# An attention and two expert-layer kernel: gates applied where results are added up, tokens stationary in the down product, sums of h left in PSUM, products of one visit interleaved

## The chip, the cores and the metric

The kernel runs on one core of a Trainium2 chip. The metric is the device time of one execution in microseconds (us); several runs were made and their median is given. A profile of one further execution gives a span, from the first to the last instruction. Engines are named as in the profile: PE is the matrix engine (its weight loads are PEld), DVE the vector engine, ACT the scalar engine, POOL the GpSimd engine, SP the engine that issues the DMAs.

## The reference

Random-feature attention, then eight dense experts gated by a Sinkhorn matrix P, then one wide layer with a swish-like activation. All is float32; 2304 tokens, width 512.

```python
x = attention(q, k, v, omega)                 # (2304, 512)
P = exp(x @ w_gate - max); 8 rounds of row and column normalization
out = 0
for e in range(8):                            # w1[e]: 512 x 1024, w2[e]: 1024 x 512
    h = np.maximum(x @ w1[e], 0.0)
    out += P[:, e:e+1] * (h @ w2[e])
h = out @ w_in                                # 512 x 2048
g = h * (1 / (1 + np.exp(-1.702 * h)))
return g @ w_out                              # 2048 x 512
```

## The kernel before

**Stages.** First attention is computed, with the products of expert 0 (done in the plain way) mixed in. Then come 54 visits. A visit takes one pair of 256-column chunks of an expert's hidden width (c is 0 or 1) and one block j of 768 tokens: 7 experts x 2 pairs x 3 blocks make 42 visits of the first layer (l = 0), and 4 pairs x 3 blocks make 12 of the second (l = 1). Every float32 operand is split in a high and a low part, so each product is three matmuls (high x high, high x low, low x high).

**Inside a visit.** Both products, up (x times w1 gives h) and down (h times w2), are done by a scheme of the Strassen-Winograd kind: 7 block products in place of 8, with sums of blocks made before and after. Q = 384 is half a block of tokens, FC = 256 a chunk. The up part (`up_fast`) makes 7 products per chunk, each 6 matmuls over 384 columns into a PSUM bank, `prod` (L1132). First products are copied by ACT to an SBUF buffer (`ring`, L1142), later ones are added to that buffer by DVE (L1147), the gate and the ReLU are applied (`gate`, L1159, times a row of gates broadcast in `gb`), and sums of the four results are made buffer by buffer (`mix`, L636 by way of `tt`). `operand` splits each of seven h operands: ACT casts the high part (L1179), DVE or POOL subtracts it for the low part (L636). The down part is `down_t` in layer 0 (L1245: w2 is stationary, h moves, 384 columns; DVE adds to `acc` in L1255) and `down_n` in layer 1 (L1269: h is stationary, w2 moves, 256 columns; L1288, or ACT's copy L1284 for the first visit of a block). In layer 1 `gate` is a sigmoid on ACT (L1168) and a product (L1174 or L636).

**The side work.** x operands come by DMA from DRAM (`load_x`, `xo`), weights come raw, are summed and split by ACT and POOL (`load_w1`, `load_w2`, `split`). w_in and w_out arrive as float64; `double_piece` turns 64 pieces of 256 columns into float32 by six DVE instructions (L1069 to L1085) and one addition, spread over the first layer. Between the layers `y_operands` makes the seven x operands of the second layer out of `acc`.

**The order.** All of this after the attention is recorded as operations with keys that they read and write. A planner (`Plan`) simulates the engines with a cost for each operation and emits every engine's instructions in the order of its simulation. Its main PE operations stay in the order in which they were recorded; for operations marked VP it also decides whether DVE or POOL does them. On the chip each engine then runs its list strictly in order and waits at semaphores. In before the visits are recorded one after the other: chunk 0 up, chunk 1 up, down.

Of the kernel before, what the change touches and what calls it, by code (L numbers as in the profile page):

```python
# [10 lines left out]
F32 = mybir.dt.float32  # L11
# [13 lines left out]
class Plan:  # L25
# [7 lines left out]
    LAT = 0.13  # L33
    BELOW = 5.0
# [58 lines left out]
    def run(self):  # L93
# [12 lines left out]
        while done < len(self.ops):  # L106
# [8 lines left out]
            for e in ("X", "PE", "DVE", "POOL", "ACT", "SP"):  # L115
# [57 lines left out]
def tile_performer_sinkhorn_moe(  # L173
# [25 lines left out]
    P = 128  # L199
# [399 lines left out]
    scr_g = dram.tile([NTILE * E, P], F32, name="scr_g")  # L599
# [11 lines left out]

    def rec(eng, dur, fn, r=(), w=(), **kw):
# [3 lines left out]
        else:  # L616
            plan.add(eng, dur, fn, r, w, **kw)
# [4 lines left out]
    def dve_us(n):  # L622
        return 0.12 + 0.00136 * n

    def ps_us(n):
        return 0.17 + 0.00103 * n
# [22 lines left out]
    acc_t = [t.rearrange("p (k n) -> p k n", n=SUP) for t in ACC]  # L649
    acc_n = [t.rearrange("p (t d) -> p t d", d=DM) for t in ACC]  # L650

    def acc_q(j, d, th):
        return acc_t[j][:, d, th * Q : (th + 1) * Q]

    def acc_keys(j):
        return [("acc", j, d, th) for d in range(NK) for th in range(2)]
# [74 lines left out]
    def e0_visit(c, j, halves, begins, ends, nxt, after, first):  # L731
# [32 lines left out]
        for th in halves:  # L764
            fs = range(NF) if th == 0 else range(NF - 1, -1, -1)
            for d in range(NK):
                o, key = free_bank(py_banks, "py")
                for m, f in enumerate(fs):

                    def fn(e, o=o, d=d, f=f, m=m, i=hs[th, f]):  # L770
                        e0_mm(o(), [w[:, f, d * P : (d + 1) * P] for w in EW], EH[i], 6, 3 * m, e)
# [3 lines left out]
                        "PE", 3 * MM, fn,  # L775
                        [("ew", f, 0), ("ew", f, 1), ("eh", i, 0), ("eh", i, 1)], [key], main=True,
                    )
                    if m:
                        a, k = acc_q(j, d, th), ("acc", j, d, th)
                        if first:  # L780
                            rec("ACT", act_us(Q), lambda e, a=a, o=o: nc.scalar.copy(a, o()), [key], [k])
                        else:
                            rec(
                                "DVE", ps_us(Q),
                                lambda e, a=a, o=o: e.tensor_tensor(out=a, in0=o(), in1=a, op=ALU.add),
                                [key, k], [k],
                            )
                        if d:
# [6 lines left out]
                    yield 3 * MM  # L795
# [26 lines left out]
    def sinkhorn():  # L822
# [643 lines left out]
```

## Time and profile before

| | |
|---|---|
| time, median of 3 runs | 2373.74 us (2370.9 to 2382.63) |
| time of the profiled execution | 2373.05 us |
| its span | 2371.3 us |
| busy PE / DVE / ACT / POOL | 89% / 83% / 39% / 65% of the span |
| mean granted PE clock | 0.965 |
| DMA | 440.76 MB, mean 186 GB/s |

The difference between time and span is what lies around the program. Busy shares are averages over stages of different kind. Matmuls are pipelined and overlap in the profile, so a busy PE isn't a PE at its peak; what a matmul takes in a dense run is read from how many start in a stretch.

### The profile page before, as it was taken

How to read it: one execution, taken by the hardware profiler on the slowest of the kernel's cores; microseconds unless marked ns; L12 is line 12 of the kernel's file. 1: busy time of each engine (PE TensorE's matmuls, PEld its weight loads, DVE VectorE, ACT ScalarE, POOL GpSimd, SP SyncE). 2: the span in 40 equal slices, each digit the busy share in tenths (PEclk: the TensorE clock that was granted, in tenths of full speed). 3: DMA queues.
4: the chain of work that ended last, by engine and by line, in shares of the span. 5: the costliest groups of instructions: out<-in, count | busy, mean ns of one | idle time of the engine just before them, and what ended most of it. 6: DMA issues, size and time to landing. Idle time of an engine off the chain costs nothing. (4 is left out here: it accounts for less than half of the span.)

```text
span 2371.3 us, 35013 instructions
## 1 busy us (share of the span) xinstructions
PE 2102.4 (89%) x12248; PEld 2005.1 (85%) x12248; DVE 1979.5 (83%) x3132; ACT 929.3 (39%) x2026; POOL 1538.9 (65%) x1341
## 2 busy tenths in 40 slices
PE   8999997788888888889888889888899877899988
PEld 8999987787878888788888888788888877888988
DVE  7666579989998998989898998988987988687777
ACT  6655533232333342333333243333333355535433
POOL 3212036767776776768776676857687877678776
PEclk9999998899999999999999999999999989999999
DMA  7333168464654654665555555645664678345444
GB/s 153 92 79 90 45 237 228 172 219 149 231 194 170 234 201 165 228 191 189 222 201 179 222 198 178 232 182 183 222 198 162 242 260 278 126 190 211 166 170 147
DMA packets 259919, 440.76 MB, mean 186 GB/s; under 512 B 74512, under 2 KB 199072, under 8 KB 259744
## 3 DMA queue, kind: packets, MB, share of 16 engines
q1 hardware_dynamic: 259744, 438.53, 54.0%
q8 instruction: 97, 1.59, 0.3%
q14 instruction: 78, 0.64, 0.1%
HBM read 392.25 MB, written 46.21 MB: 185 GB/s over the span
## 5 line engine op out<-in xcount | busy, mean ns | idle before, releaser
L1132 PE MATMUL bank<-xo,w 128*128 128x384 f32 x4536 | 846.8, 342 | 123.7 <-DVE ring L1147 68.9
L1132 PEld LDWEIGHTS bank<-xo,w 128*128 128x128 f32 x4536 | 796.0, 191 | 163.0 <-DVE ring L1147 88.7
L1245 PE MATMUL bank<-h,w 128*128 128x384 f32 x3528 | 675.5, 347 | 82.4 <-DVE h L636 38.5
L636 POOL TENSOR_TENSOR h<-ring,h 128x384 fp32r<-128x384 f32 x471 | 561.5, 1205 | 271.5 <-ACT h L1179 198.6
L1245 PEld LDWEIGHTS bank<-h,w 128*128 128x128 f32 x3528 | 635.0, 195 | 118.5 <-DVE h L636 51.9
L1179 ACT CAST h<-ring 128x384 fp32r<-128x384 f32 x756 | 378.9, 513 | 541.3 <-DVE ring L636 248.7
L636 POOL TENSOR_TENSOR w<-raw,w 128x512 fp32r<-128x512 f32 (+1 forms) x216 | 349.6, 1632 | 60.2 <-ACT w L1048 60.1
L1142 ACT COPY ring<-bank 128x384 f32<-128x384 f32 x324 | 154.5, 478 | 555.8 <-PE bank L1132 546.7
L1255 DVE TENSOR_TENSOR acc<-bank,acc 128x384 f32<-128x384 f32 x588 | 301.9, 548 | 51.6 <-PE bank L1245 50.2
L636 DVE TENSOR_TENSOR h<-ring,h 128x384 fp32r<-128x384 f32 x285 | 293.9, 1044 | 7.2 <-ACT h L1179 5.4
L636 DVE TENSOR_TENSOR ring<-ring,ring 128x384 f32<-128x384 f32 (+1 forms) x285 | 292.2, 1029 | 2.0 <-POOL ring L636 0.2
L1147 DVE TENSOR_TENSOR ring<-bank,ring 128x384 f32<-128x384 f32 x324 | 177.7, 550 | 123.1 <-PE bank L1132 117.6
L636 POOL TENSOR_TENSOR ring<-ring,ring 128x384 f32<-128x384 f32 (+1 forms) x171 | 208.8, 1224 | 50.8 <-DVE ring L1159 26.3
L1159 DVE SCALAR_TENSOR_TENSOR ring<-ring,gb 128x384 f32<-128x384 f32 x252 | 232.3, 924 | 10.8 <-DMA gb<-scr_g 8.4
L1269 PE MATMUL bank<-w,h 128*128 128x256 f32 x1512 | 203.8, 297 | 32.5 <-DVE h L636 18.5
L1269 PEld LDWEIGHTS bank<-w,h 128*128 128x128 f32 x1512 | 198.1, 204 | 38.2 <-DVE h L636 20.5
L636 POOL TENSOR_TENSOR raw<-raw 128x256 f32<-128x256 f32 x262 | 217.2, 844 | 16.1 <-DMA raw<-in_moe_w_dram 12.5
L696 POOL TENSOR_TENSOR egl<-raw,egh 128x512 fp32r<-128x512 f32 x32 | 41.1, 1303 | 204.2 <-ACT egh L693 194.4
L1048 ACT CAST w<-raw 128x768 fp32r<-128x768 f32 (+1 forms) x216 | 148.2, 691 | 62.3 <-PE bank L1132 28.6
L1288 DVE TENSOR_TENSOR acc<-bank,acc 128x256 f32<-128x256 f32 x216 | 77.9, 414 | 31.3 <-PE bank L1269 24.3
L387 ACT ACTIVATE feat<-pj,nb 128x128 f32<-128x128 f32 x272 | 73.9, 386 | 66.8 <-DVE nb L383 66.6
L636 POOL TENSOR_TENSOR ring<-ring,gb 128x384 f32<-128x384 f32 x35 | 37.5, 1077 | 71.2 <-ACT gb L1168 71.2
(245 smaller groups left out, 2232.1 us busy)
## 6 DMA issues: line engine op xcount, KB each, us to landing
xo<-sx SPq DMA_DIRECT2D x378, 768.0 KB, 7.5
raw<-in_moe_w_dram SPq DMA_DIRECT2D x288, 128.0 KB, 2.4
sx<-ring SPq DMA_DIRECT2D x48, 192.0 KB, 3.4
gb<-scr_g SPq DMA_DIRECT2D x24, 384.0 KB, 8.0
raw<-in_moe_w_dram SPq DMA_DIRECT2D x16, 512.0 KB, 3.4
f64r<-in_moe_w_in_dram SPq DMA_DIRECT2D x32, 256.0 KB, 3.9
f64r<-in_moe_w_out_dram SPq DMA_DIRECT2D x32, 256.0 KB, 2.9
sx<-acc SPq DMA_DIRECT2D x42, 192.0 KB, 4.4
```

The source lines that it names most:

```text
L387: nc.scalar.activation(f[:, h, :], pvs[h // 4][:, h % 4, :], AF.Exp, bias=nb[:, h : h + 1])
L636: lambda e: e.tensor_tensor(out=out(), in0=a(), in1=b(), op=op),
L1048: lambda e, a=a, b=b: nc.scalar.copy(T[w, c, 0][:, a:b], r[:, a:b]), raws, [(w, c, g, 0)],
L1132: nc.tensor.matmul(o(b), T["w1", c, a][:, slot, kk], T["xo"][x][:, y, kk], start=start and kk == 0 and n == 0, stop=kk == 1 and n == 2, sk ...
L1142: rec("ACT", act_us(Q), lambda e: nc.scalar.copy(RT(i), o(b)), [("b", b)], [("ring", i)])
L1147: lambda e: e.tensor_tensor(out=RT(i), in0=o(b), in1=RT(i), op=ALU.add),
L1159: lambda e: e.scalar_tensor_tensor(out=RT(i), in0=src(), scalar=0.0, in1=g(), op0=ALU.max, op1=ALU.mult),
L1179: rec("ACT", act_us(Q), lambda e: nc.scalar.copy(T["h", c, a, 0], RT(i)), [("ring", i)], [("h", c, a, 0)])
L1245: nc.tensor.matmul(bank[i][:, :Q], T["w2", c, x][:, slot, d * P : (d + 1) * P], T["h", c, a, y], start=start and c == 0 and m == 0, stop=c ...
L1255: lambda e, q=q, i=i: e.tensor_tensor(out=q, in0=bank[i][:, :Q], in1=q, op=ALU.add),
L1269: nc.tensor.matmul(bank[i][:, u], T["h", c, a, x][:, t * P : (t + 1) * P], T["w2", c, y][:, slot], start=start and t % 2 == 0 and c == 0 a ...
L1288: lambda e, q=q, i=i, u=u: e.tensor_tensor(out=q, in0=bank[i][:, u], in1=q, op=ALU.add),
```

## The change

- **Gates** are no longer multiplied into h. In layer 0 ReLU is all that h gets; the gate of a token multiplies the result when it is added to `acc` (one DVE instruction with the gate as a per-partition factor). `gb`, its DMAs (`load_gates`, 24 of 384 KB) and the broadcast are gone. Expert 0's gate is applied by ACT.
- **Down product**: tokens are stationary in both layers, `acc` holds tokens by rows throughout. The old `down_t` goes; 126 matmuls of 256 columns stand in place of its 84 of 384. Expert 0's down product is turned as well (512 columns). `y_operands` therefore transposes `acc` on PE first, and is cut in three units per block.
- **Sums of h stay in PSUM**: ACT copies the first product to the next bank (PSUM to PSUM) and matmuls accumulate on it; DVE adds bank and ring into a bank; the casts and the low parts read the bank; three of the sums read a bank and one ring. One sum per chunk stays ring by ring.
- **First down product**: ACT copies its three results to the banks where the second one accumulates, and DVE adds only the accumulated sums.
- **Woven order**: `up_fast` and `down` are generators; the two chunks' products alternate, the first down turn comes before the last up product, and the last down turn of a visit comes after the first up product of the next.
- **float64 pieces**: 32 of 512 columns in place of 64 of 256, the final addition always on POOL.
- **The planner's costs** change (DVE instructions on SBUF dearer, hand-over time 0.17).

```diff
-    LAT = 0.13
-    BELOW = 5.0
+    LAT = 0.17
+    BELOW = 2.5
...
     def dve_us(n):
-        return 0.12 + 0.00136 * n
+        return 0.17 + 0.0022 * n
...
     def gate_rows(j):
-        for d in range(NK):
-            a = acc_t[j][:, d, :]
...
+        for t in range(ST):
+            a, g = acc_n[j][:, t], pg[:, ST * j + t, 0:1]
+            rec(
+                "ACT", act_us(DM), lambda e, a=a, g=g: nc.scalar.activation(a, a, AF.Copy, scale=g),
...
+    def y_operands(j, u, b0):
+        plan.haste = plan.clock + (2.0, 3.0, 3.0)[u], (0.14, 0.14, 0.2)[u]
+        for b, t in ((b0, u), (b0 + 1, u + 3)):
+            def fn(e, b=b, t=t):
+                for kk in range(NK):
+                    nc.tensor.transpose(
+                        bank[b][:, kk * P : (kk + 1) * P], acc_n[j][:, t, kk * P : (kk + 1) * P], ident
+                    )
...
     def up_fast(l, p, j, c):
-        le, ri, pc = ((0, 1, 2), (3, 4, 2))[c]
-        m1, u2, m5, r21, s1, s2 = range(6 * c, 6 * c + 6)
+        le, ri, pc, q = ((0, 1, 2, 7), (3, 4, 2, 7))[c]
+        r11, u2, r22, n3, s1, s2 = range(6 * c, 6 * c + 6)
...
         prod(le, 0, 0, True)
-        copy(m1, le)
-        prod(pc, 2, 3, True)
-        add(m1, pc)
-        gate(m1, 0)
-        operand(A11, m1)
-        prod(le, 3, 2, False)
-        copy(u2, le)
+        act(lambda: o(pc), lambda: o(le), [("b", le)], [("b", pc)])
+        yield
         prod(ri, 1, 1, True)
-        copy(m5, ri)
+        act(lambda: RT(r22), lambda: o(ri), [("b", ri)], [("ring", r22)])
+        for slot in (3, 2) if c == 0 else (2, 3):
+            if slot == 3:
+                prod(le, 3, 2, False)
+                act(lambda: RT(u2), lambda: o(le), [("b", le)], [("ring", u2)])
+                continue
+            prod(pc, 2, 3, False)
+            if l:
+                swish(pc)
+            operand(A11, bank_of(pc), True, r11)
+        yield
         prod(le, 5, 4, False)
-        add(m5, le)
-        gate(m5, 1)
+        dve(bank_of(q), bank_of(le), ring_of(r22), ALU.add)
+        if l:
+            swish(q)
+        operand(A22, bank_of(q), True, r22)
+        tt(lambda: RT(s2), lambda: RT(r22), lambda: RT(r11), ALU.subtract, Q, [("ring", r22), ("ring", r11)], [("ring", s2)])
         prod(ri, 4, 5, False)
-        add(u2, ri)
-        gate(u2, 0)
-        operand(A12, u2)
+        dve(bank_of(ri), bank_of(ri), ring_of(u2), ALU.add)
+        if l:
+            swish(ri)
+        operand(A12, bank_of(ri), True)
+        yield
         prod(le, 6, 6, False)
-        gate(r21, 1, le)
-        mix(s1, r21, m5, ALU.add)
-        mix(r21, r21, m1, ALU.subtract)
-        mix(s2, r21, m5, ALU.add)
+        if l:
+            swish(le)
+        mixed(s2, le, s2, ALU.add)
+        mixed(s1, le, r22, ALU.add)
+        mixed(n3, le, r11, ALU.subtract)
...
-        mix(u2, u2, s2, ALU.subtract)
-        operand(S4, u2)
-        operand(A22, m5)
+        mixed(u2, ri, s2, ALU.subtract)
+        operand(S4, ring_of(u2))
...
+    PLACES = {
+        "C": ((5, 0), (5, 1), (6, 0)),
+        "D": ((0, 0), (2, 0), (1, 0)),
+        "E": ((7, 0), (7, 1), (6, 1)),
+    }
...
+                if n == 0:
+                    d = PLACES["D"][t][0]
+                    rec(
+                        "ACT", act_us(FC),
+                        lambda e, i=i, d=d, u=u: nc.scalar.copy(bank[d][:, 0:FC], bank[i][:, u]),
+                        [("b", i, half)], [("b", d)],
+                    )
+                    continue
...
+                    g = pg[:, ST * j + m, e : e + 1]
+                    rec(
+                        "DVE", ps_us(FC),
+                        lambda e, q=q, i=i, u=u, g=g: e.scalar_tensor_tensor(
+                            out=q, in0=bank[i][:, u], scalar=g, in1=q, op0=ALU.mult, op1=ALU.add
+                        ),
...
     def all_visits():
+                ups = [up_fast(l, p, j, c) for c in range(2)]
                 load_x(l, j)
+                next(ups[0])
+                for _ in last or ():
+                    pass
...
+                next(ups[0])
+                next(ups[1])
+                next(ups[0])
+                next(ups[1])
+                for _ in ups[0]:
+                    pass
...
+                next(ups[1])
+                last = down(l, e, j, l and p == 0, l and not more)
+                next(last)
+                for _ in ups[1]:
+                    pass
...
+                for _ in range(len(TURNS[l]) - 2):
+                    next(last)
```

What the planner makes of it in a middle visit of layer 0. DVE in before, from the sum of one product to the sums of h (names: `bank` PSUM, `ring` SBUF, `gb` gates, `h031` the low part of operand 3 of chunk 0, `f64r` and `f64w` the float64 work):

```order
L1147 TENSOR_TENSOR ring6_3911<-bank2_3889,ring6_3911 128x384 [waits PE_49,Activation_49]
L636 TENSOR_TENSOR h031_4789<-ring4_3909,h030_4788 128x384 [waits Activation_49]
L1159 SCALAR_TENSOR_TENSOR ring6_3911<-ring6_3911,gb_4500 128x384 [waits DVE_49]
L1069 TENSOR_SCALAR f64w_4502<-f64r_4501 128x256 [waits DMAHW1_49]
L1073 SCALAR_TENSOR_TENSOR f64w_4502<-f64r_4501,f64w_4502 128x256 [waits DVE_49]
L1147 TENSOR_TENSOR ring8_3913<-bank3_3890,ring8_3913 128x384 [waits PE_49,Activation_49]
L1076 TENSOR_SCALAR f64w_4502<-f64r_4501 128x256 [waits DMAHW2_49]
L1159 SCALAR_TENSOR_TENSOR ring8_3913<-ring8_3913,gb_4500 128x384 [waits DVE_49]
L1147 TENSOR_TENSOR ring7_3912<-bank4_3891,ring7_3912 128x384 [waits PE_49]
L1159 SCALAR_TENSOR_TENSOR ring9_3914<-bank3_3890,gb_4500 128x384 [waits PE_49]
L1159 SCALAR_TENSOR_TENSOR ring7_3912<-ring7_3912,gb_4500 128x384 [waits DVE_49]
L636 TENSOR_TENSOR ring10_3915<-ring9_3914,ring8_3913 128x384 [waits DVE_49]
```

DVE in the change at the same place (L1173 adds bank and ring into a bank, L1211 makes a low part out of a bank, L1184 a sum out of a bank and a ring, `stage` is the float64 work, now 512 wide):

```order
L1173 TENSOR_TENSOR bank7_3773<-bank0_3766,ring2_3786 128x384 [waits DVE_49,PE_49]
L1082 TENSOR_SCALAR stage_4180<-stage_4180 128x512 [waits DMAHW0_49,Pool_49]
L1211 SCALAR_TENSOR_TENSOR h061_4560<-bank7_3773,h060_4559 128x384 [waits Activation_49]
L1173 TENSOR_TENSOR bank1_3767<-bank1_3767,ring1_3785 128x384 [waits PE_49]
L1086 SCALAR_TENSOR_TENSOR stage_4180<-stage_4180 128x512 [waits DVE_49]
L1211 SCALAR_TENSOR_TENSOR h101_4564<-bank2_3768,h100_4563 128x384 [waits Activation_49]
L1211 SCALAR_TENSOR_TENSOR h011_4550<-bank1_3767,h010_4549 128x384
L1184 SCALAR_TENSOR_TENSOR ring4_3788<-bank0_3766,ring2_3786 128x384 [waits PE_49]
L1184 SCALAR_TENSOR_TENSOR ring5_3789<-bank0_3766,ring5_3789 128x384 [waits Pool_49]
L1184 SCALAR_TENSOR_TENSOR ring3_3787<-bank0_3766,ring0_3784 128x384
L1173 TENSOR_TENSOR bank7_3773<-bank3_3769,ring8_3792 128x384 [waits DVE_49,PE_49]
```

Nearly every row of DVE now has one operand in PSUM, and the gate's rows are gone.

PE in before, from the last product of a visit (`xo6`) to the first down product, which follows at once:

```order
L1132 MATMUL bank3_3890<-xo6_3904,w111_4499 128x384
L1132 MATMUL bank3_3890<-xo6_3904,w110_4498 128x384
L1245 MATMUL bank5_3892<-h000_4782,w200_4780 128x384
L1245 MATMUL bank5_3892<-h001_4783,w200_4780 128x384 [waits Pool_49]
L1245 MATMUL bank5_3892<-h000_4782,w201_4781 128x384
L1245 MATMUL bank6_3893<-h000_4782,w200_4780 128x384
L1245 MATMUL bank6_3893<-h001_4783,w200_4780 128x384
L1245 MATMUL bank6_3893<-h000_4782,w201_4781 128x384
L1245 MATMUL bank7_3894<-h030_4788,w200_4780 128x384
```

PE in the change, from the end of the first down turn (chunk 0, `h001`) over the last up product to the second down turn (chunk 1, `h100`):

```order
L1294 MATMUL bank6_3772<-w200_4545,h001_4548 128x256
L1152 MATMUL bank3_3769<-xo6_3783,w110_4178 128x384 [waits DVE_49]
L1152 MATMUL bank3_3769<-xo6_3783,w111_4179 128x384
L1152 MATMUL bank3_3769<-xo6_3783,w110_4178 128x384 x2
L1152 MATMUL bank3_3769<-xo6_3783,w111_4179 128x384
L1152 MATMUL bank3_3769<-xo6_3783,w110_4178 128x384
L1294 MATMUL bank5_3771<-w210_4561,h100_4563 128x256
L1294 MATMUL bank5_3771<-w211_4562,h100_4563 128x256
L1294 MATMUL bank5_3771<-w210_4561,h101_4564 128x256
```

The first down turn has moved ahead of the last up product.

PE in the change two turns later, where the third tile of turn `h03` goes into the second half of bank 6, whose first half ACT copies away:

```order
L1294 MATMUL bank7_3773<-w200_4545,h030_4553 128x256
L1294 MATMUL bank7_3773<-w201_4546,h030_4553 128x256
L1294 MATMUL bank7_3773<-w200_4545,h031_4554 128x256
L1294 MATMUL bank6_3772<-w200_4545,h030_4553 128x256 [waits Activation_49]
L1294 MATMUL bank6_3772<-w201_4546,h030_4553 128x256
L1294 MATMUL bank6_3772<-w200_4545,h031_4554 128x256
L1294 MATMUL bank0_3766<-w200_4545,h010_4549 128x256
```

The two halves of bank 6 belong to different sums, and yet the later one waits for the reader of the earlier.

## Rows read from the trace of the kernel before

**Rows 1.** Windows: the four stretches of visits; busy us, clock, DMA share, GB/s.

```profile
core 0: us, PE busy (x) PEld busy (x) DVE busy (x) ACT busy (x) POOL busy (x), PEclk, DMA share, GB/s
420.00:545.50 125.50, 101.10 (x501) 94.52 (x500) 111.84 (x154) 36.75 (x73) 87.12 (x70) 0.90 0.53 187
545.50:1938.00 1392.50, 1223.82 (x6558) 1159.17 (x6557) 1256.94 (x1895) 478.93 (x963) 1006.37 (x869) 0.97 0.57 201
1938.00:2098.60 160.60, 132.58 (x841) 126.63 (x841) 117.34 (x163) 81.47 (x182) 118.36 (x101) 0.93 0.61 218
2098.60:2366.80 268.20, 250.74 (x1682) 246.54 (x1680) 202.86 (x341) 118.90 (x248) 197.12 (x169) 0.96 0.46 172
```

**Rows 2.** Source line L1132: min/median/max ns, first and last start; idle until (us, times).

```profile
L1132 PE MATMUL bank<-xo,w x4536: 331/334/689, 420.0 to 2350.1; 128*128 128x384 f32 x198
...
  DMA xo<-sx: 1.7, 2
```

**Rows 3.** Timeline of three visits: start us, us, engine, line, names, count.

```profile
1014.35 12.71 PE L1132 MATMUL bank<-xo,w 128*128 128x384 f32 x72
1015.64 0.48 ACT L1142 COPY ring<-bank 128x384 f32<-128x384 f32 x1 [8.58 <-PE bank L1132]
...
2319.12 5.55 PE L1269 MATMUL bank<-w,h 128*128 128x256 f32 x45
2325.37 10.30 PE L1269 MATMUL bank<-w,h 128*128 128x256 f32 x81 [0.70 <-DVE acc L1288]
```

**Rows 4.** Windows: three single visits (layer 0, layer 0, layer 1).

```profile
1014.30:1047.50 33.20, 30.00 (x170) 29.01 (x169) 28.53 (x49) 9.50 (x20) 23.79 (x23) 1.00 0.64 208
...
1082.30:1119.20 36.90, 32.42 (x169) 30.30 (x169) 36.27 (x54) 12.88 (x26) 30.58 (x28) 0.95 0.64 214
...
2304.40:2335.50 31.10, 30.34 (x213) 29.76 (x211) 23.34 (x43) 12.96 (x28) 19.89 (x17) 1.00 0.65 242
```

**Rows 5.** Waits of PE from 545.5 to 1938: us in total, times, longest.

```profile
PE bank L1132 <- DVE ring L1147: 52.0, 38, 3.8
PE bank L1132 <- ACT ring L1142: 42.5, 47, 2.7
PE bank L1245 <- DVE h L636: 36.2, 33, 2.0
PE bank L1245 <- DVE acc L1255: 28.8, 40, 3.2
```

**Rows 6.** Groups by line and form, 545.5 to 1938: busy us, mean ns | idle before.

```profile
L636 POOL TENSOR_TENSOR h<-ring,h 128x384 fp32r<-128x384 f32 x344 | 410.2, 1204 | 240.3 <-ACT h L1179 171.5 <-PE bank L1132 68.5
...
L1159 DVE SCALAR_TENSOR_TENSOR ring<-ring,gb 128x384 f32<-128x384 f32 x234 | 216.7, 928 | 2.4
L636 DVE TENSOR_TENSOR h<-ring,h 128x384 fp32r<-128x384 f32 x202 | 204.2, 1024 | 5.9 <-ACT h L1179 5.1
...
L1147 DVE TENSOR_TENSOR ring<-bank,ring 128x384 f32<-128x384 f32 x234 | 128.2, 549 | 66.1 <-PE bank L1132 60.8 <-ACT ring L1142 3.5 <-ACT h L1179 1.6
L1142 ACT COPY ring<-bank 128x384 f32<-128x384 f32 x234 | 111.6, 478 | 433.1 <-PE bank L1132 425.3 <-POOL ring L636 2.3 <-DVE f64w L1079 1.5
...
L1073 DVE SCALAR_TENSOR_TENSOR f64w<-f64r,f64w 128x256 uint32<-128x256 uint32 x59 | 45.6, 774 | 0.9
...
L1076 DVE TENSOR_SCALAR f64w<-f64r 128x256 uint32<-128x256 uint32 x59 | 31.7, 538 | 0.0
```

**Rows 7.** Source lines L636, L1147, L1288 on DVE: min/median/max ns, first and last start.

```profile
L636 DVE TENSOR_TENSOR h<-ring,h x285: 541/1081/2189, 438.9 to 2356.7; 128x384 fp32r<-128x384 f32 x143
...
L1147 DVE TENSOR_TENSOR ring<-bank,ring x324: 540/546/559, 423.0 to 2349.6; 128x384 f32<-128x384 f32 x162
...
L1288 DVE TENSOR_TENSOR acc<-bank,acc x216: 406/413/426, 1976.5 to 2367.2; 128x256 f32<-128x256 f32 x108
```

**Rows 8.** Groups by line and form, whole span: ACT's copy of 256 columns, PE's transposes.

```profile
L1284 ACT COPY acc<-bank 128x256 f32<-128x256 f32 x36 | 11.7, 377 | 24.2 <-PE bank L1269 24.2
...
L461 PEld LDWEIGHTS xt<-ident,x 128*128 128x128 f32 x72 | 8.8, 144 | 0.5
```

More of the change, by code (lines that the diff above doesn't have):

```diff
@@ L610, in tile_performer_sinkhorn_moe, with spread @@
     live = [True]
+    def spread(keys):
+        return [h for k in keys for h in ([k + (0,), k + (1,)] if k[0] == "b" and len(k) == 2 else [k])]
     def rec(eng, dur, fn, r=(), w=(), **kw):
@@ L648, in tile_performer_sinkhorn_moe, with o_keys @@
     ACC = [cst.tile([P, NK * SUP], F32, name=f"acc{j}") for j in range(NB)]
-    acc_t = [t.rearrange("p (k n) -> p k n", n=SUP) for t in ACC]
     acc_n = [t.rearrange("p (t d) -> p t d", d=DM) for t in ACC]
[L652 to L656, printed above, removed]
+    def o_keys(j, t):
+        return [("o", j, t, dh) for dh in range(2)]
     e0 = opened(e0_pool, "e0", "left")
@@ L1012, in load_w1 @@
         src = scr_in[c] if l else w1[e][:, c * FC : (c + 1) * FC].rearrange("(k p) f -> p k f", p=P)
-        rd = [("scr", 0, c)] if l else []
+        rd = [("scr", 0, c, kk) for kk in range(NK)] if l else []
         for (f, kh), o in W1SLOT.items():
@@ L1024, in load_w2 @@
         src = scr_out[c] if l else w2[e][c * FC : (c + 1) * FC, :].rearrange("(k p) f -> p k f", p=P)
-        rd = [("scr", 1, c)] if l else []
+        rd = [("scr", 1, c, f) for f in range(NF)] if l else []
         for (f, dh), o in W2SLOT.items():
@@ new lines, in operand @@
+        def operand(a, src, psum=False, kept=None):
+            h, g = (lambda: T["h", c, a, 0]), (lambda: T["h", c, a, 1])
+            hk, gk = ("h", c, a, 0), ("h", c, a, 1)
+            f = AF.Relu if psum and l == 0 else AF.Copy
+            act(h, src[0], [src[1]], [hk], f)
+            if kept is not None:
+                act(lambda: RT(kept), src[0], [src[1]], [("ring", kept)], f)
+            if not psum:
+                tt(g, src[0], lambda: h().bitcast(F32), ALU.subtract, Q, [src[1], hk], [gk])
+            elif l:
+                dve((g, gk), src, ((lambda: h().bitcast(F32)), hk), ALU.subtract)
+            else:
@@ L1318, in all_visits @@
     def all_visits():
+        ended, last = [], None
         for pi, (l, e, p) in enumerate(pairs):
@@ L1352, in switch_x @@
                 T["w1", c, a] = r.tile([P, 7, 2, P], F32R, name=f"w1{c}{a}")
-        T["gb"] = r.tile([P, N], F32, name="gb")
-        for k in ("f64r", "f64w"):
-            T[k] = r.tile([P, 2 * FC], F32, name=k)
+        T["stage"] = r.tile([P, 10 * FC], F32, name="stage")
+        for k in ("sig0", "sig1"):
+            T[k] = r.tile([P, Q], F32, name=k)
     def switch_e0():
```

353 lines of the change are left out of this document (170 added, 183 removed).

## The prediction

> **What bounds the kernel now.** I read the windows of the stages first, then the rate of dense matmuls, then who PE waits for, then what the engine it waits for does.
>
> The first product starts at 420.0 us [rows 2]; the rest of the span, 82% of it, is 54 visits in four stretches [rows 1]: 3 visits of 41.8 us, 39 of 35.7 (1392.5 / 39), 4 of 40.2 around the change of layer, 8 of 33.5, and 4.5 us behind them. Before 420 the change touches little, so the visits decide.
>
> What would a visit take if PE never waited? In a dense run 72 matmuls of 384 columns take 12.71 us, the last one's overlap of 0.34 [rows 2] left off: 12.37 / 71 = 0.174 us each. 45 of 256 columns take 5.55: 5.27 / 44 = 0.120 [rows 3]. A visit of layer 0 has 168 of the first kind: 29.2 us. So 6.5 us of 35.7 are lost, 253 us in the 39 visits. The reader is to see two kinds of loss. One is waiting: PE waits for sums that DVE makes (L1147, L636), for banks that DVE or ACT hasn't read (L1255, L1142) [rows 5]. The other follows from it: the granted clock is 0.97 in that stretch [rows 1], 1.00 in a visit of 33.2 us and 0.95 in one of 36.9 [rows 4]. Time at half clock costs half of itself, so 0.03 of 1392 us, 42 us, goes there.
>
> Why is DVE late? It is busy 1256.9 of 1392.5 us, 90%, 32.2 us per visit [rows 1], and its list is in order. Much of that is instructions with both inputs in SBUF: 1.02 us for a low part, 0.93 for a gate, against 0.55 for the same 384 columns when one input is a bank [rows 6]. The minima are alike, 541 and 540 ns; the median with SBUF inputs is 1081, with a bank 546 [rows 7]. POOL works on SBUF 72% of that time [rows 1]; I read the difference as POOL's.
>
> **The change, part by part.**
>
> PE. 84 up matmuls x 0.174 + 126 down x 0.120 = 14.6 + 15.1 = 29.7 us, in both layers: 0.5 more than now in layer 0. The new floor is the old one.
>
> DVE, counted from the planner's list (visits 6 to 30). 18 additions of 256 columns to acc: 0.414 now [rows 7]; with a factor per partition not in the trace, between 0.41 and 0.55 (the form with 384 columns); I take 0.414: 7.5 us. 18 instructions of 384 columns with a bank as input x 0.549 = 9.9. Four of these write a bank, which no row shows: between 0.54 and 1.02, I take 0.55, since one input is still a bank. 2.4 instructions with two SBUF inputs x 1.02 = 2.5 (the list gives 7.6 more of this kind to POOL). The float64 work: 0.86 pieces per visit of six wide instructions. Six narrow ones now take 3.97 together, from 0.774 to 0.538 [rows 6]; twice as wide they cost between the same and twice, 4.0 to 7.9; I take 6.0, the middle: 5.2 per visit. Sum 25.1 against 32.2, with bounds of 23.3 (1.8 less for the pieces) and 31.0 (2.4 + 1.9 + 1.6 more for additions, writes to banks and pieces).
>
> [...]
>
> POOL now makes 8.8 low parts a visit (344 in 39) and sums beside; the list leaves it 7.6 pair instructions in all, so at least 1.2 x 1.20 = 1.4 us less than its 25.8 [rows 6, 1]. ACT makes 24 casts and copies of 384 columns and 3 of 256, for 20 of 384 now: 4 x 0.48 + 3 x 0.38 = 3.0 us on 12.3 [rows 6, 8, 1]. Its copy from bank to bank is in no row; between 0.38 and 0.52, I take 0.48; ACT has the room. Gates for expert 0 go to ACT as well, and 24 DMAs of 384 KB go. DMA must carry 201 x 35.7 / 31.4 = 229 GB/s; one visit of 31.1 us carries 242 now [rows 4]. All of this lies beside PE.
>
> What stays on PE's path is hand-over, and the weave decides how much. I walk one visit through the four lists with the durations above and 0.25 us from a product's last start to its reader (the copy at 1015.64 behind six matmuls from 1014.35 [rows 3]). At t = 0 the first product starts. Everything in the first 12 us is early: the copy to the second bank has 2 us of other products in front of its use. Four places remain. (1) Chunk 1's fifth product waits for ACT's copy of bank 3, seven ACT instructions behind the product: 0.3. (2) Turn h03's third tile in bank 6 waits for the three ACT copies of 0.38 behind the turn before: 0.45. (3) The same tile for chunk 1 waits for three additions of 0.41: 0.5. (4) Turn h05's third tile waits likewise: 0.45. Places 2 to 4 exist because a wait is for the whole bank, not the half. Sum 1.7, so a visit takes 31.4. This is also what short visits take now: 31.1 us for 29.7 of matmuls [rows 4]. While DVE is 25 of 31.4 us busy it is never more than about 1 us late at these places. If all but 0.8 of the waits vanish, a visit takes 30.5; if each of the three DVE places comes 0.5 later, 33.
>
> The ends. First product: 418, bounds 412 to 425 (the same x operands come first; the gate products leave DVE and POOL). The first three visits have 3 x (41.8 - 35.7) = 18 us over the rest now [rows 1], from DVE's backlog; with less work I take 8 (0 to 18). The change of layer has 4 x (40.2 - 33.5) = 27 over; its new form adds 72 transposes of 0.144 [rows 8] = 10 us of PE, but about halves DVE's pair work; I take 12 (5 to 27). The end keeps 4.5.
>
> Sum of the span: 418 + 54 x 31.4 (1695.6) + 8 + 12 + 4.5 = 2138. The profiled execution took 2373.05 for its span of 2371.3, 1.75 more, and its time is 0.7 under the median of the runs. That gives **2140 us**, 234 us less. The planner's new costs have no price of their own; they are in the lists that I counted.
>
> **Rivals.**
>
> A, the lists meet with hardly a wait. PE's four places shrink to 0.6 us because ACT and DVE run ahead, the first visits and the layer change cost 10 together: 30.3 x 54 + 418 + 10 + 6 = 2070. For it: places 1 and 2 hang on 0.3 to 0.5 us. Against: short visits now, with fewer hand-overs, still lose 1.4 us.
>
> B, DVE stays the bound. At its upper bound of 31.0 us and today's share of 0.903 a visit takes 34.3 where the float64 pieces run: 39 x 2.9 = 113 more, 2253. For it: the wide pieces stand in front of low parts in the list, one waiting for a DMA and a POOL addition. Against: all upper ends would have to hold at once.
>
> C, slower than before: the shared banks. Five turns a visit have a tile in bank 6 or 5 that waits for the reader of the previous sum, and PE's list is in order, so everything behind it waits. The waits of this kind are 3.2 us at the longest now (L1255) [rows 5]. From 4.3 us per visit more than I take, about 0.9 at each, the gain is gone; at 1.2 each a visit takes 37.4 and the time is 2140 + 54 x 6 = 2464. For it: DVE must finish low parts, conversions and additions in one list. Against: DVE's load falls by a fifth.
>
> D, no change: the weave moves the waits of L1147 and L1142 to others of equal size, 35.7 a visit, 2372. It needs DVE's load to be no cause, against 90% busy.
>
> **How the numbers follow.** The forecast, 2105 to 2205 (30.8 to 32.6 a visit): 0.60. A: 0.15. B: 0.14. C: 0.05. D: 0.03. Something else that leaves a smaller gain: 0.03. The range 2080 to 2235 holds the forecast, the nearer half of A and most of what lies towards B, about 0.8. Half a per cent, 12 us, is about what a measurement of this kernel can tell from no change. Faster: 0.60 + 0.15 + 0.14 + 0.03 = 0.92; the same 0.03; slower 0.05.
>
> **What the profile of the change would show.** Right: visits of 31 to 32 us with 210 matmuls, DVE 75 to 82% busy in the middle, clock 0.99 or more there, PE's waits under 2.5 us a visit and in the name of the additions to acc and of ACT's copies from bank to bank. DVE's instructions on banks at 0.41 and 0.55. Wrong: wide float64 instructions above 1.3 us each, bank-writing additions near 1 us (both B); waits over 1 us at bank 6 and a clock of 0.95 (C); a first product after 430. The prediction would also be wrong if x operands landed late in the shorter visits: waits of the up products for `xo`, which are 1.7 us in two places now [rows 2].

## The result, and the profile after

The change takes 2135.98 us in the median (2134.32 to 2139.32, four runs), against 2372.55 for the kernel before: a ratio of 0.8997 [0.8969, 0.9024], 237 us less. The forecast was 2140. The profiled execution of the change took 2134.32 us, its span is 2132.6.

The page's first part, busy us, share of the span and instructions of each engine in the change:

```profile
span 2132.6 us, 38364 instructions
...
PE 2054.1 (96%) x13938; PEld 1977.8 (93%) x13938; DVE 1484.8 (70%) x2962; ACT 1050.4 (49%) x2444; POOL 1149.9 (54%) x1086
```

Windows of the change (they answer to [rows 1]): the first visit, the next 39, the three around the change of layer, the last eleven but for their end.

```profile
398.30:441.00 42.70, 32.91 (x208) 31.85 (x207) 35.37 (x72) 27.50 (x53) 29.92 (x28) 0.88 0.53 183
441.00:1661.80 1220.80, 1193.12 (x8193) 1165.10 (x8192) 847.91 (x1684) 546.16 (x1209) 744.50 (x691) 1.00 0.60 219
1661.80:1779.90 118.10, 103.58 (x704) 99.93 (x703) 89.43 (x198) 71.38 (x180) 57.76 (x56) 0.96 0.91 284
1779.90:2128.10 348.20, 340.44 (x2321) 330.42 (x2319) 237.57 (x494) 194.84 (x451) 173.63 (x164) 1.00 0.53 191
```

A middle visit takes 1220.8 / 39 = 31.3 us where it took 35.7, at a granted clock of 1.00 for 0.97. DVE is busy 21.7 us a visit there (847.9 / 39), 69% of the time, for 32.2 and 90%.

Groups of the change by line and form in the same 39 visits (they answer to [rows 6]): busy us, mean ns, idle before.

```profile
L1329 DVE SCALAR_TENSOR_TENSOR acc<-bank,lg,acc 128x256 f32<-128x256 f32 x703 | 296.8, 478 | 190.5 <-PE bank L1294 189.7
L639 POOL TENSOR_TENSOR h<-ring,h 128x384 fp32r<-128x384 f32 x237 | 258.7, 1115 | 81.1 <-ACT h L1162 79.2 <-DVE ring L1184 1.2
L1184 DVE SCALAR_TENSOR_TENSOR ring<-bank,ring 128x384 f32<-128x384 f32 x312 | 160.1, 548 | 18.7 <-PE bank L1152 18.1 <-POOL ring L639 0.3
...
L1211 DVE SCALAR_TENSOR_TENSOR h<-bank,h 128x384 fp32r<-128x384 f32 x234 | 127.4, 553 | 115.8 <-ACT ring L1162 99.1 <-ACT h L1162 15.1
...
L1173 DVE TENSOR_TENSOR bank<-bank,ring 128x384 f32<-128x384 f32 x156 | 87.5, 562 | 26.1 <-PE bank L1152 24.1
L639 DVE TENSOR_TENSOR h<-ring,h 128x384 fp32r<-128x384 f32 x75 | 73.5, 992 | 19.9 <-ACT h L1162 19.4
...
L1311 ACT COPY bank<-bank 128x256 f32<-128x256 f32 x117 | 37.8, 365 | 43.2 <-PE bank L1294 40.7 <-DVE ring L1184 2.0
L1162 ACT ACTIVATE bank<-bank 128x384 f32<-128x384 f32 x78 | 37.0, 475 | 354.1 <-PE bank L1152 336.9 <-DVE h L1211 10.5 <-DVE stage L1082 6.7
```

The reader is to see that low parts out of a bank take 553 ns and those left with two SBUF inputs still 992; and that DVE's idle time now ends mostly at PE's products (189.7 us in front of the additions alone), else at ACT's copies. L1184, the sums out of a bank and a ring, runs 8 times a visit (312 / 39): four sums a chunk are of this kind, where the section on the change says three.

Waits of PE in the change (they answer to [rows 5]; the first three are of the whole span, the last two of 441.0 to 1661.8): us in total, times, longest.

```profile
PE bank L1294 <- DVE acc L1329: 28.4, 101, 0.6
PE bank L1294 <- DVE stage L972: 10.8, 2, 6.6
...
PE bank L1294 <- ACT bank L1311: 2.0, 6, 0.8
```

```profile
PE bank L1294 <- DVE acc L1329: 27.0, 97, 0.5
PE bank L1152 <- ACT ring L1162: 0.6, 3, 0.2
```

DVE's sums and low parts (L1147, L636) and ACT's copies stopped PE for 131 us in the 39 visits before; 0.6 us of ACT's copies is left of that. What stops PE in the middle now has one name. The timeline of a visit shows it (start us, us, engine, line, names, count):

```profile
1027.68 2.46 DVE L1329 SCALAR_TENSOR_TENSOR acc<-bank,lg,acc 128x256 f32<-128x256 f32 x6 [1.25 <-PE bank L1294]
...
1029.00 3.61 PE L1294 MATMUL bank<-w,h 128*128 128x256 f32 x27 [0.28 <-DVE acc L1329]
1031.57 1.27 DVE L1329 SCALAR_TENSOR_TENSOR acc<-bank,lg,acc 128x256 f32<-128x256 f32 x3 [1.43 <-PE bank L1294]
...
1032.89 2.42 PE L1294 MATMUL bank<-w,h 128*128 128x256 f32 x18 [0.28 <-DVE acc L1329]
1034.27 1.27 DVE L1329 SCALAR_TENSOR_TENSOR acc<-bank,lg,acc 128x256 f32<-128x256 f32 x3 [1.43 <-PE bank L1294]
...
1035.60 0.62 PE L1294 MATMUL bank<-w,h 128*128 128x256 f32 x3 [0.28 <-DVE acc L1329]
```

Three additions end at 1031.57 + 1.27 = 1032.84, and PE starts again at 1032.89. The idle time shown is 0.28 us, but a stop costs more: the 18 matmuls from 1032.89 on and the next stop take until 1035.60, 2.71 us where 18 x 0.120 would be 2.16, so some 0.55. This visit has three stops; the 39 visits have 97, or 2.5 a visit, which make 1.4 of the 1.6 us by which a visit is over its 29.7. By the order of PE's list they stand at the third tiles of the turns h13, h05 and h06 (37, 33 and 27 times), each in one half of bank 6 while DVE still reads the other half.

### The profile page after: what moved, and what is told of

Same layout as the page of the kernel before. It is cut to its first block, busy times and chain, and to the rows that moved or that the text cites. A ratio compares the mean times of both kernels' runs of the same rounds, so it can differ in the third digit from the quotient of the medians.

```text
span 2132.6 us, 38364 instructions
## 1 busy us (share of the span) xinstructions
PE 2054.1 (96%) x13938; PEld 1977.8 (93%) x13938; DVE 1484.8 (70%) x2962; ACT 1050.4 (49%) x2444; POOL 1149.9 (54%) x1086
## 4 chain that ended last, share of the span: by engine, by line
PE 79%; DVE 14%; ACT 2%; issue 2%; DMA 2%; POOL 1%; SPq 0%; DVEq 0%; ACTq 0%; POOLq 0%
PE bank L1152 34%; PE bank L1294 31%; DVE acc L1329 6%; PE ph L716 3%; PE py L773 3%; PE num L431 2%; DVE ring L639 1%; DMA sx<-stage 1%; PE kv L401 1%; DVE acc L1322 1%; DVE h L639 1%; PE pt L342 1%; DVE bank L1173 1%; PE pj L367 1%; PE pj L368 1%
## 5 line engine op out<-in xcount | busy, mean ns | idle before, releaser
L1294 PE MATMUL bank<-w,h 128*128 128x256 f32 x6804 | 892.8, 286 | 47.9 <-DVE acc L1329 28.4
L1294 PEld LDWEIGHTS bank<-w,h 128*128 128x128 f32 x6804 | 848.4, 191 | 86.4 <-DVE acc L1329 49.7
L639 POOL TENSOR_TENSOR w<-raw,w 128x768 fp32r<-128x768 f32 (+1 forms) x216 | 327.5, 1524 | 313.4 <-ACT w L1058 302.6
L1329 DVE SCALAR_TENSOR_TENSOR acc<-bank,lg,acc 128x256 f32<-128x256 f32 x756 | 319.5, 478 | 200.8 <-PE bank L1294 200.0
L639 POOL TENSOR_TENSOR h<-ring,h 128x384 fp32r<-128x384 f32 x321 | 348.5, 1107 | 133.9 <-ACT h L1162 130.1
L1162 ACT ACTIVATE ring<-bank 128x384 f32<-128x384 f32 x432 | 210.2, 491 | 132.5 <-PE bank L1152 125.9
L1162 ACT ACTIVATE h<-ring 128x384 fp32r<-128x384 f32 x432 | 207.1, 527 | 87.4 <-DVE ring L1184 63.2
L1211 DVE SCALAR_TENSOR_TENSOR h<-bank,h 128x384 fp32r<-128x384 f32 x252 | 137.2, 552 | 120.5 <-ACT ring L1162 103.5
L1162 ACT ACTIVATE h<-bank 128x384 fp32r<-128x384 f32 x324 | 157.6, 492 | 62.8 <-DVE bank L1173 34.9
L1184 DVE SCALAR_TENSOR_TENSOR ring<-bank,ring 128x384 f32<-128x384 f32 x336 | 172.4, 548 | 20.6 <-PE bank L1152 20.0
L1173 DVE TENSOR_TENSOR bank<-bank,ring 128x384 f32<-128x384 f32 x216 | 120.9, 561 | 30.4 <-PE bank L1152 27.9
L639 DVE TENSOR_TENSOR h<-ring,h 128x384 fp32r<-128x384 f32 x111 | 112.0, 1024 | 22.4 <-ACT h L1162 21.9
L1173 DVE TENSOR_TENSOR bank<-bank,sig 128x384 f32<-128x384 f32 x96 | 53.5, 561 | 50.1 <-ACT sig L1162 48.8
```

Source lines behind the costliest of these rows:

```text
L639: lambda e: e.tensor_tensor(out=out(), in0=a(), in1=b(), op=op),
L1162: rec("ACT", act_us(Q), lambda e: nc.scalar.activation(out(), src(), f, **kw), r, w)
L1173: lambda e: e.tensor_tensor(out=out[0](), in0=a[0](), in1=b[0](), op=op), [a[1], b[1]], [out[1]],
L1184: lambda e: e.scalar_tensor_tensor(out=RT(out), in0=o(b), scalar=0.0, in1=RT(c), op0=ALU.max, op1=op),
L1211: lambda e: e.scalar_tensor_tensor(out=g(), in0=src[0](), scalar=0.0, in1=h().bitcast(F32), op0=ALU.max, op1=ALU.subtract),
L1294: nc.tensor.matmul(bank[i][:, u], T["h", c, a, x][:, t * P : (t + 1) * P], T["w2", c, y][:, slot], start=start and half == 0 and c == 0 an ...
```

## The experiments

Theory: a middle visit was lost to DVE's late sums, and these were late because instructions with two SBUF inputs are dear beside POOL; with the sums in PSUM and the products woven, PE is stopped only at shared banks. Rivals: the weave alone does it; less DVE load alone does it; the planner's costs do it.

### One half each: seq and weave_only

seq is the change with its visits recorded one after the other:

```diff
-                next(ups[0])
-                next(ups[1])
-                next(ups[0])
-                next(ups[1])
-                for _ in ups[0]:
+                for _ in up_fast(l, p, j, 0):
                     pass
...
+                for _ in up_fast(l, p, j, 1):
                     pass
...
-                for _ in range(len(TURNS[l]) - 2):
-                    next(last)
+                for _ in down(l, e, j, l and p == 0, l and not more):
+                    pass
```

> The change with its visits recorded one after the other again (chunk 0 up, chunk 1 up, down, nothing carried over), all else kept. Theory (PE sets the pace, and it takes both the smaller DVE load and the weave to keep it fed): the last sums of h are late for the down part, a visit takes about 33 us in place of 31.3, 2200 to 2290 in all. Rival 1 (DVE's smaller load is the whole gain): 2125 to 2150. Rival 2 (the weave is the whole gain): 2330 or more.

2204.77 us (2204.33 to 2206.17), ratio 0.9286 [0.9272, 0.9299], in the theory's band, but not by its mechanism: PE hardly waits for h at the down part. It waits for ACT's copies to a ring at the up products (below). weave_only is the kernel before with its `up_fast` and down parts cut by `yield` and recorded in the woven order, nothing else (its first lines):

```diff
         copy(m5, ri)
+        yield
         prod(le, 5, 4, False)
...
+                next(ups[0])
+                next(ups[1])
+                next(ups[0])
+                next(ups[1])
```

> The kernel before with the weave alone: up generators and down turns interleaved as in the change, gates, SBUF sums and down product as before (the last down turn isn't carried over at the three visits that make the operands of layer 2). Theory: DVE's 32.2 us a visit stay, so a visit falls from 35.7 to about 34.5 and no further, 2290 to 2350 in all, DVE over 92% busy in the middle. Rival 1 (DVE's load is the whole gain): 2360 to 2385. Rival 2 (the weave is the whole gain): under 2200.

2374.77 us (2371.39 to 2386.66), ratio 1.0006 [0.999, 1.0021]: no change; the expectation of 2290 to 2350 fell, and DVE is 88% busy in the middle where over 92% was expected. The time lies in the band of rival 1, but DVE's load isn't the whole gain either, since seq has the smaller load and lacks 69 us of the change. Waits of PE, first in seq, whole span, then in weave_only from 545.5 to 1938 as in [rows 5]:

```profile
PE bank L1152 <- ACT ring L1162: 36.3, 54, 2.6
PE bank L1294 <- DVE acc L1329: 32.6, 117, 0.6
```

```profile
PE bank L1250 <- DVE h L636: 106.8, 73, 4.3
...
PE bank L1132 <- DVE ring L1147: 16.6, 13, 2.5
...
PE bank L1132 <- ACT ring L1142: 1.4, 3, 0.5
```

The weave takes L1147's waits from 52.0 [rows 5] to 16.6 and L1142's from 42.5 to 1.4, and low parts that DVE makes late now stop PE for 106.8 us where it was 36.2; all rows of this list together make 162 us where they made 166.5. By the order of PE's list most of these stops are at two down turns of chunk 1 (h11 and h12); the first turn, which the weave brings forward, doesn't wait for low parts. The wait has moved from some results of a busy DVE to others. So the other parts alone are worth 170 us, the weave alone nothing, the weave on top of them 69: the parts' gains don't add up one by one.

### Is it DVE's load? conv_twice and before_no_gate

conv_twice does each float64 step twice:

```diff
-        for i, s in enumerate(steps):
-            rec("DVE", us, s, R + W, W, due=at + 8.0 + 4.0 * i)
+        for i, s in enumerate(steps + steps):
+            rec("DVE", us, s, R + W, W, due=at + 8.0 + 2.0 * i)
```

> The change with the six float64 steps of each piece done twice on DVE (the second time over the same data), which adds some 4 us of DVE to each of about 36 visits: 28.5 of 31.3 us. Theory (PE is the bound and DVE has room): 2136 to 2165. Rival (DVE's list still sets the pace): the added time shows in full, 36 x 4 = 144 us, 2250 to 2290.

2139.4 us (2137.93 to 2141.7), ratio 0.9013 [0.8997, 0.9028], in the theory's band. Window of visits 2 to 40, DVE the third busy column:

```profile
446.30:1665.50 1219.20, 1193.38 (x8193) 1167.10 (x8192) 1003.75 (x1878) 554.85 (x1209) 772.14 (x681) 1.00 0.60 219
```

156 us more DVE work, 4.0 a visit, and the 39 visits take 1219.2 us for 1220.8. DVE's load no longer sets the pace. before_no_gate goes the other way, in the kernel before:

```diff
             if l == 0:
+                if b is not None:
+                    copy(i, b)
+                return
```

> The kernel before without the gate instructions of layer 0 (gate and ReLU of experts 1 to 7 are left out; the product that the gate took from its bank is copied by ACT). It takes some 6.7 us of DVE a visit away and nothing else. Theory (DVE's load is what the change lowers to gain, and 7 us of it are enough to show): a visit falls by 3 to 4.5 us in 42 visits, 2185 to 2250. Rival (the gain comes from sums read in PSUM, whatever the load): 2330 to 2370.

2293.39 us (2288.11 to 2294.62), ratio 0.9654 [0.9635, 0.9673], between the two expectations. Window from 545.5 over the length of 39 visits, and two of PE's waits in it:

```profile
545.50:1860.00 1314.50, 1192.32 (x6511) 1152.21 (x6512) 1061.74 (x1597) 503.68 (x1034) 946.99 (x846) 0.98 0.57 210
```

```profile
PE bank L1132 <- DVE ring L1147: 53.5, 30, 3.7
...
PE bank L1132 <- ACT ring L1142: 13.4, 18, 2.6
```

DVE falls from 90% to 81% busy (1061.7 / 1314.5), and the wait for L1147 doesn't fall with it (52.0 in [rows 5]); the one for ACT's copies does (42.5 there). A visit there is 33.7 us long (39 of them lie between 463.7 and 1778.6), so DVE is busy 27.2: half of the 10.5 us that the change takes from it gives 80 of its 237 us. That the rest comes from shorter hand-overs, further ahead of their use, is argued from the lists; no run has it alone.

### Why were DVE's instructions dear? low_from_ring and pool_cut

low_from_ring makes four of the low parts out of the copy in SBUF:

```diff
+            elif kept is not None:
+                dve((g, gk), ring_of(kept), ((lambda: h().bitcast(F32)), hk), ALU.subtract)
             elif l:
```

> The change with four of a visit's low parts (A11 and A22 of both chunks) made by DVE out of the copy in SBUF in place of the bank, so with both inputs in SBUF. Theory (two SBUF inputs beside POOL are dear, about 1.0 us against 0.55): the mean of these instructions is 0.9 to 1.1 us, DVE has about 1.9 us more a visit (26.5 of some 32), the low parts are later by ACT's second copy as well, and the time is 2145 to 2185. [...]

2140.77 us (2139.37 to 2143.07), ratio 0.9 [0.8977, 0.9022]. pool_cut is the same with POOL's pair instructions cut:

```diff
+    def pair(e, out, a, b, op):
+        if e is nc.gpsimd:
+            spare["pool"] = spare.get("pool", 0) + 1
+            if 250 < spare["pool"] < 800:
+                out, a, b = out[..., :16], a[..., :16], b[..., :16]
+        e.tensor_tensor(out=out, in0=a, in1=b, op=op)
```

> low_from_ring once more, in the same order of every list, with POOL's pair instructions from the 251st to the 799th cut to their first 16 columns; the other columns of these low parts, weight sums and float64 sums are left out. DVE's instructions keep their sizes, so this tells whether POOL's work is what makes DVE's instructions with two SBUF inputs dear (there 540 at least, 694 in the median, 879 ns in the mean). Theory (POOL is it): where POOL is cut, their mean is 540 to 620 ns, those with a bank as input stay at 546 to 560, the wide float64 steps fall from 4.3 us for six to under 3.6, and the time falls by 0 to 15 us against low_from_ring, to 2125 to 2141, since DVE has room. Rival (it is ACT's or the DMAs' traffic in SBUF, which stays): the mean stays at 800 to 900 ns and the time within 5 us of low_from_ring.

2137.1 us (2136.6 to 2141.19), ratio 0.8986 [0.8965, 0.9007]. Groups on DVE from 700 to 1500 us, first of low_from_ring, then of pool_cut (7 lines further down in its code):

```profile
L1184 DVE SCALAR_TENSOR_TENSOR ring<-bank,ring 128x384 f32<-128x384 f32 x208 | 106.5, 546 | 6.4 <-PE bank L1152 5.8
L1173 DVE TENSOR_TENSOR h<-ring,h 128x384 fp32r<-128x384 f32 x103 | 90.9, 883 | 44.6 <-ACT ring L1162 44.4
...
L639 DVE TENSOR_TENSOR h<-ring,h 128x384 fp32r<-128x384 f32 x50 | 50.0, 1005 | 6.3 <-ACT h L1162 6.2
...
L1082 DVE TENSOR_SCALAR stage<-stage 128x512 uint32<-128x512 uint32 x22 | 13.1, 597 | 0.0
```

```profile
L1191 DVE SCALAR_TENSOR_TENSOR ring<-bank,ring 128x384 f32<-128x384 f32 x208 | 107.3, 549 | 18.1 <-PE bank L1159 17.3
L1180 DVE TENSOR_TENSOR h<-ring,h 128x384 fp32r<-128x384 f32 x104 | 61.1, 587 | 56.6 <-ACT ring L1169 56.6
...
L639 DVE TENSOR_TENSOR h<-ring,h 128x384 fp32r<-128x384 f32 x50 | 29.4, 592 | 11.1 <-ACT h L1169 11.0
...
L1089 DVE TENSOR_SCALAR stage<-stage 128x512 uint32<-128x512 uint32 x22 | 9.2, 418 | 0.0
```

DVE's instructions are the same in both; POOL alone is cut, from 510 to 155 busy us of these 800, while ACT (355 and 358 us) and the DMA share (0.61 and 0.62) stay. The forms with two SBUF inputs fall from 883 and 1005 ns to 587 and 592, the form with a bank stays (546, 549). So it is POOL that makes them dear, as [rows 6, 7] were read; in the kernel before itself POOL was never cut. The times, 4 us apart, can't tell theory from rival here. In low_from_ring the mean of 883 ns is just under the theory's band (900 to 1100), and the time is 4 us under its band (2145 to 2185), since the theory forgot what conv_twice had shown: DVE has the room.

A bank isn't the dearer input here: the form with a bank takes 549 ns with POOL cut and the one with two SBUF inputs 587, beside the uncut POOL 546 and 883. The last row of each list, a float64 step, has one SBUF input and yet falls from 597 to 418 ns, where the sums out of a bank and a ring, with one SBUF input too, stay; what makes this difference no run here shows.

### What is left at the shared banks: bank6_first, bank6_all, seq_bank6

bank6_first lets a C turn begin with the tile in bank 6 that was its third:

```diff
-            for t in range(3):
+            for t in (2, 0, 1) if b == "C" else range(3):
```

> The change with the three tiles of the C turns of the down product in the order 2, 0, 1, so that bank 6, which C and E share, is written and read first. Theory (what a visit loses over 29.7 us is mostly the wait of E's third tile for the reader of C's third tile in the same bank): two waits of 0.45 to 0.55 us a visit vanish, 30.4 us a visit, 2075 to 2100 in all. Rival (PE waits because DVE is late as such): the waits move to other tiles, 2125 to 2145.

**2088.9 us** (2088.23 to 2089.93), ratio 0.8797 [0.8784, 0.881], faster than both kernels. Its window of the 39 visits, and the waits of PE in its whole span:

```profile
441.80:1623.00 1181.20, 1171.32 (x8192) 1158.82 (x8191) 864.36 (x1688) 546.41 (x1210) 743.76 (x688) 1.00 0.62 226
```

```profile
PE bank L1294 <- DVE stage L972: 9.7, 4, 3.8
PE bank L1294 <- ACT bank L1311: 7.0, 21, 1.4
...
PE bank L1294 <- DVE acc L1329: 1.6, 6, 0.5
```

As the theory had it: 30.3 us a visit, which is 40 of the 47 us won, and the wait for the additions falls from 28.4 us to 1.6. Between a C tile in bank 6 and the next E tile in its other half there are now four tiles, where there were two. Where a C turn follows an E turn, its first tile goes to bank 6 before the addition that reads E's half has begun, and PE doesn't wait; that this addition then waits for PE is likely, and not measured. All turns in this order:

```diff
-            for t in range(3):
+            for t in (2, 0, 1):
```

> The change with all down turns (C, D and E) taking their third tile first, not only C's. Theory (what is left after the order 2, 0, 1 in C's turns is the wait of a C turn's first tile for E's tile in the other half of bank 6, which now is the last of its turn): E's tile in bank 6 is read two tiles earlier, the rest of 0.54 us a visit falls to about 0.3, 2070 to 2085 us. Rival (E's first tile then itself comes right behind a C turn whose tile in bank 6 is read two tiles before, 0.24 to 0.36 us of matmuls against an addition of 0.48): the wait moves to E's turns, 2088 to 2105.

2109.72 us (2107.14 to 2110.0), ratio 0.8865 [0.8847, 0.8883]: 21 us worse than C's turns alone, in the rival's direction and 5 past its band. In the middle PE waits for the additions again:

```profile
PE bank L1294 <- DVE acc L1329: 7.3, 30, 0.5
```

Again only two tiles lie between a C tile and the E tile in the same bank, as in the change. The 39 visits take 1192.9 us for 1181.2, 12 of the 21 us; the others lie mostly behind the change of layer. And the order of C's turns in the sequential kernel, seq:

> The change with its visits recorded one after the other, not woven, and C's tiles in the order 2, 0, 1. Theory (the two waits are independent: of the 3.05 us that a visit of the sequential order loses, some 1.5 us are at bank 6's tiles and go with the order, 1.2 us are up products that wait for ACT's copy to a ring and stay): 2115 to 2150, 55 to 90 us less than the sequential order had, and the weave is worth 30 to 60 us on top of the new tile order. Rival (DVE and ACT are late for other reasons in the sequential order, and PE is stopped at the next hand-over when bank 6 doesn't stop it): 2170 to 2205.

2141.43 us (2140.98 to 2142.62), ratio 0.9001 [0.8983, 0.9019], as the theory had it: the waits for the additions go, those for ACT's rings stay (35.7 us in 54 waits for 36.3 in seq). On this order the weave is worth 53 us (2141.4 less 2088.9).

### A dear factor, a moved unit, the old costs

gate_one adds with a constant 1 in place of the gate:

```diff
-                            out=q, in0=bank[i][:, u], scalar=g, in1=q, op0=ALU.mult, op1=ALU.add
+                            out=q, in0=bank[i][:, u], scalar=1.0, in1=q, op0=ALU.mult, op1=ALU.add
```

> The change with the constant 1 in place of the token's gate in layer 0's additions (the gates of experts 1 to 7 are left out). It measures the price of a factor per partition by itself: the additions took 478 ns with it. Theory (the factor costs the 64 ns over the 414 of a plain addition, and it costs time where three additions stand before a wait at bank 6): additions back at about 415 ns, two or three waits a visit 0.15 shorter, 2115 to 2130. Rival (the additions lie beside PE): 2132 to 2140, whatever they take.

2116.04 us (2115.58 to 2118.89), ratio 0.8916 [0.8902, 0.8929], in the theory's band. The additions as min/median/max ns, in the change and in gate_one:

```profile
L1329 DVE SCALAR_TENSOR_TENSOR acc<-bank,lg,acc x756: 466/476/488, 432.5 to 1741.5; 128x256 f32<-128x256 f32 x189
```

```profile
L1329 DVE SCALAR_TENSOR_TENSOR acc<-bank,acc x756: 405/414/426, 432.4 to 1720.6; 128x256 f32<-128x256 f32 x189
```

A factor per partition costs 62 ns. Without it PE's wait for the additions falls from 28.4 us to 0.9, and 20 us of the time go. y_later moves the y work around the change of layer behind both up parts of a visit:

```diff
-                if ended:
-                    y_operands(ended[0], 1, 5)
                 next(ups[1])
...
                 if ended:
+                    y_operands(ended[0], 1, 3)
                     y_operands(ended.pop(), 2, 3)
```

> The change with the second unit of each block's layer-2 operands moved behind both up parts, to banks 3 and 4, ahead of the third unit there. Theory (the visits at the change of layer are long because the first down turn waits up to 6.6 us for bank 5, which the second unit holds): those waits go, 8 to 14 us less, 2121 to 2129. Rival (these visits are long because of the units' work on DVE and ACT): 2133 to 2140.

2141.14 us (2137.88 to 2141.85), ratio 0.9016 [0.9003, 0.903]. The wait for L972 is gone and the three visits take 121.4 us for 118.1: new waits for ACT's ring (3.5 at the longest) and for the transposes' operands (4.1) took its place. The theory falls. The time is 1 us past the rival's band; that the units' work on DVE and ACT makes these visits long fits, and isn't shown by itself. old_costs gives the planner its old constants, and 0.05 again between PE's own operations:

```diff
-    LAT = 0.17
-    BELOW = 2.5
+    LAT = 0.13
+    BELOW = 5.0
...
-        return 0.17 + 0.0022 * n
+        return 0.12 + 0.00136 * n
```

> The change with the planner's old costs (hand-over 0.13, slack 5.0, cheap SBUF instructions on DVE), so that only the order of the lists and the split between DVE and POOL differ. Theory (the load and the weave make the gain; the lists have room): 2130 to 2165. Rival (the planner's truer costs are a main part of the gain): 2190 or more.

2154.53 us (2149.68 to 2155.1), ratio 0.9071 [0.9056, 0.9085], in the theory's band: 19 us of the 237 are the planner's costs.

## Why the prediction was right, step by step

- **What bounds the kernel.** Right: PE waited for late sums, and with the waits the clock's loss went too: 1.00 in the 39 visits for 0.97. The half clock that the prediction reckons with is in the trace of the kernel before: from 1101.0 to 1104.0 us, behind a stop of 2.19 us, the granted clock is 0.50, and six matmuls of 384 columns take 2.29 us there where six take 1.21 at 1036.05 in the change. That waiting lowers the clock is read from such stretches and not shown by itself. That DVE's load is a cause before is shown by before_no_gate, and POOL's price on two SBUF inputs by pool_cut, in the new kernel; that this price made DVE late in the old one is read from [rows 6, 7] and not shown by itself. No wait for `xo` is among PE's.
- **A visit of 31.4.** Measured 31.3. The sum of its four places (1.7, with 1.6 measured) was right by luck in parts. By the starts of PE's matmuls, (3) and (4), the third tiles of h13 and h05, cost 0.5 and 0.45 us a visit, as forecast. (1), chunk 1's fifth product behind ACT's copy, costs nothing to speak of (0.6 us in 39 visits for ACT's rings), and (2), turn h03 behind ACT's copies, 0.1 for 0.45. A fifth of the same kind, h06's third tile behind E's additions, was missed; its 0.4 takes their place.
- **The additions.** Taken 0.414, measured 0.478: 1.2 us more DVE a visit, and the reason why three of them are late at each stop. The bound of 0.55 held.
- **The wide float64 pieces.** Taken 6.0, measured 1004 + 888 + 822 + 547 + 541 + 513 ns = 4.3 us, near the lower bound. Writes to a bank 0.56 for 0.55. With 31 pieces in 39 visits they cost 3.4 us a visit for 5.2 taken; the additions' 1.2 more make up for most of that.
- **DVE's share.** 75 to 82% was forecast, the windows say 69%: they count overlapping neighbours once. 703 additions at 478 ns are 336 us, and their row has 296.8 us busy. By durations a visit's DVE work is 24.2 us, 77%, for the 25.1 of the sum. The 32.2 us that the prediction set beside its 25.1 is a busy time; by durations it is 35.2.
- **First product.** 418 (412 to 425) taken, 398.3 measured, outside its bounds: I took the stage before it as untouched, but expert 0's down product was turned too. From 300 us on, PE's waits on DVE there fall from 17.6 us to 7.4 and its clock rises from 0.89 to 1.00. Which edit does it was not tried; 7.6 of the 20 us are the planner's costs (405.9 in old_costs).
- **First visits.** 8 taken, 42.7 - 31.3 = 11.4 measured, all in the first.
- **The change of layer.** 12 taken, 118.1 - 3 x 31.3 = 24.2 measured. The transposes were counted (10 us, 8 by the starts of PE's); the 10.8 us for which PE waits for y's sums (L972) and the clock of 0.96 in these visits were not.
- **The sum.** 398.3 + 54 x 31.3 + 11.4 + 24.2, 3.9 more in the last eleven visits and 4.5 at the end make the span of 2132.6: 20 us too many at the front, 16 too few at the two ends of the first layer. That these nearly cancel is luck.
- **Rivals.** A's visit of 30.3 us is reached by bank6_first, by the order of three tiles, not by DVE and ACT running ahead. B is refuted by conv_twice. C's mechanism is there, at 0.55 in 2.5 places a visit and not 0.9 more at each of five. D is what the weave does by itself.

## What to carry to other kernels

Ask of a sum first how many of its inputs lie in SBUF while POOL works: with a bank as one input DVE took 546 ns beside a POOL 64% busy and 549 beside one 19% busy, with two in SBUF 883 and 587. An order that brings a consumer forward gave nothing here while the engine that feeds it was 90% busy, and 53 to 69 us once it wasn't, so relieve that engine first and count the parts together. Where two sums share a bank, put as many other tiles as you can between the two that lie in it: first in C's turns and last in E's gave 47 us here, first in both only 26.

## What the runs showed of the hardware

- A per-partition factor in a DVE instruction of 256 columns out of PSUM costs 62 ns (476 for 414).
- Two SBUF inputs at 384 columns cost 587 ns in the mean with POOL cut to 19% busy, and 883 beside a POOL that is 64% busy (700 to 1500 us), at most 1973 in the whole span.
- With one input in a bank, DVE writes 384 columns to a bank in 562 ns and to SBUF in 548. ACT copies 384 columns from bank to bank in 475 ns, 256 in 365.
- Six float64 steps over 512 columns take 4.3 us beside a POOL 61% busy; over 256 columns they took 3.97 in the kernel before, beside one 72% busy. With POOL cut the wide six take 3.4 (743 + 735 + 687 + 442 + 422 + 418 ns).
